# Four row tiles of the first norm from a second copy of x with channels on partitions, and another order of additions in the mixing's third phase

## The chip, the cores and the metric

One NeuronCore of a Trainium2 chip runs the whole block as one program. The metric is device time in microseconds (us), the median of several executions. Engines work side by side, each on its own list of instructions in a fixed order: TensorE (PE; its weight loads are shown apart as PEld), VectorE (DVE), ScalarE (ACT), GpSimd (POOL), and SyncE (SP), which here issues nearly all DMA transfers. They wait for each other by semaphores. TensorE's results go to PSUM, which this kernel uses as eight tiles (banks) of 128 x 512 float32 values; the other tiles lie in SBUF, 128 partitions wide.

## The reference

A transformer block with modulated norms, sequence 2048, width 448, 16 heads of 28, all in float32. Cut to what matters:

```python
mod = (silu(c) @ w_mod).reshape(1, 6, 1, -1)
sa, ca, ga, sb, cb, gb = (mod[:, i] for i in range(6))
h = layernorm(x) * (1 + ca) + sa                  # the first norm
x = x + ga * attention(h, wqkv, wo)               # 16 heads of 28
h = layernorm(x) * (1 + cb) + sb                  # the second norm
z = gelu(h @ w_in)                                # 2048 x 1792, two halves
z1, z2 = z[..., :896], layernorm(z[..., 896:])
g = w_sp @ z2 + b_sp[:, None]                     # 2048 x 2048: the mixing
x = x + gb * ((z1 * g) @ w_out)
```

## The kernel before

**Split operands.** Most operands of matmuls are kept as two tiles of the type fp32r: hi, a rounded copy, and lo, what the rounding left out. A product then takes hi x hi, lo x hi and hi x lo. The 448 channels fill three chunks of 128 and one of 64; the last holds hi in partitions 0 to 63 and lo in 64 to 127. `STEPS` is the order of the eleven matmuls of one output tile: their first index names the part of the activations (0, 1, 2 hi; 3, 4, 5 lo; 6 both of the last chunk), and runs 0, 2, 0, 2, 3, 5, 1, 1, 4, 6, 6.

**Stages.** First norm with the projections to Q, K and V; attention, head after head; output projection with the second norm; the two halves of z; the mixing; the last product. The program's order on each engine is the order of the code: nothing is reordered by a planner.

**The first norm.** Sequence rows come in four groups of 512 (four row tiles of 128). For a group, `ln_stat` takes mean and variance per row on VectorE, `ln_rs` makes 1/sqrt(var + eps) on GpSimd, `ln_norm` subtracts and scales on VectorE (rows on partitions; the last 64 channels are written twice, the second time by ScalarE). `ln_transpose` then turns the group on TensorE, sixteen 128 x 128 transposes into four PSUM banks, one per chunk of channels (L118). From each bank ScalarE makes scale ca and offset sa (L125) and the hi part (L132), and VectorE the lo part (L85). The result, `hT[g]`, has channels on partitions and feeds V (`v_tile`, one row tile, eleven matmuls, L273, then a copy by ScalarE, L277) and Q and K (`qk_unit`, one block of 128 rows of Q or K for one group, eleven matmuls, L288, then hi by ScalarE, L303, lo by VectorE, and two stores to DRAM, L309). Group 0 goes another way: `h_hi`, `h_off`, `h_lo` make hi straight from the transposed bank (L391), then offset minus hi (L397), and lo from the two (L401).

`ln_next(g)` is called while the tiles of group g - 1 are multiplied: it takes the statistics of the group after, transposes group g, and normalises the group after. Each loop round g = 1, 2, 3 is: two V tiles of group g, `ln_next(g + 1)`, two more V tiles, then the units m = 0 and 3 of the group. In round 3 these units come first, together with the clearing of the padded rows of the stacked Q and K tiles (L518 to L520) and the loads of head 0 (L529, L531).

**Banks.** Seven of the PSUM banks are dealt out by `bank` in a fixed cycle of two tags, s (three banks) and m (four); `turn` counts. A tile that gets a bank waits until the last reader of the bank's former tile is done.

**The mixing.** The 2048 x 2048 product is done with seven block products of one level of Strassen's scheme, in four phases p = 0 to 3, each in two halves of the output columns, each half in eight steps. In a step of phases 0 to 2 each of seven accumulators `acc[0..6]` gets three matmuls (L1224, L1225, L1226), in the order 0 to 6; in phase 3 there are four, 0, 1, 2, 6. After the eighth step `evac` adds the accumulators to the result blocks u11, u22 and so on (L1230 on VectorE), while TensorE begins the next half in new banks of the cycle. In phase 2 acc[0], acc[1], acc[2] are each added twice (u11 and u22), acc[3] to acc[5] once (u22), acc[6] once.

Of the kernel before, what the change touches and what calls it, by code (L numbers as in the profile page):

```python
# [8 lines left out]
F32 = mybir.dt.float32  # L9
F32R = mybir.dt.float32r  # L10
AF = mybir.ActivationFunctionType
ALU = mybir.AluOpType
# [4 lines left out]
S, D, H, DH, FH = 2048, 448, 16, 28, 896  # L17
# [3 lines left out]
NG = 4  # L21
# [9 lines left out]


@with_exitstack
def tile_adaln_mha_gmlp(ctx, tc, x, wqkv, wo, w_in, w_spT, b_sp, w_out, cT, w_mod, w_late, out):
    nc = tc.nc
    ctx.enter_context(tc.manual_schedule())
    pe, dve, act, pool, sp = nc.tensor, nc.vector, nc.scalar, nc.gpsimd, nc.sync
# [7 lines left out]
    m_scr = scr.tile([H, 2, S], F32, name="m_scr")  # L45
# [5 lines left out]
    ident = const.tile([128, 128], F32, name="ident")  # L51
# [6 lines left out]
    cols = {}  # L58
# [11 lines left out]
    hT = [hview(heapD[g // 2], g % 2 * 3584, 7, 512) for g in range(NG)]  # L70
# [35 lines left out]
    def rstd_of(var, rs, n):  # L106

        pool.tensor_scalar(out=rs, in0=var, scalar1=EPS, scalar2=None, op0=ALU.add)
        pool.tensor_tensor(out=rs, in0=rs, in1=mhalf[:, :n], op=ALU.pow)
# [35 lines left out]
    turn = [0]  # L145
# [12 lines left out]
    e1 = early.enter_context(tc.tile_pool(name="e1", bufs=2))  # L158
# [5 lines left out]
    def bank(name, kind=None):  # L164

        if kind is None:
            kind = "smsmsmm"[turn[0] % 7]
            turn[0] += 1
        return ring.tile([128, 512], F32, name=name, tag=kind, bufs=3 if kind == "s" else 4)
# [69 lines left out]
    mv1, xn1 = {}, {}  # L239

    def ln_stat(g, ts):
        if g not in mv1:
            mv1[g] = e1.tile([128, 4, 2], F32, name="mv"), e1.tile([128, 4], F32, name="rs")
        for t in ts:
            st = e1.tile([128, 6], F32, name="st", bufs=4)
            dve.bn_stats(out=st, in_=xts[4 * g + t])
            dve.bn_aggr(out=mv1[g][0][:, t, :], in_=st)

    def ln_rs(g, a, e):
        mv, rs = mv1[g]  # L250
        rstd_of(mv[:, a:e, 1], rs[:, a:e], e - a)

    def ln_norm(g, ts):
        mv, rs = mv1[g]
        for t in ts:
            xn = e1.tile([128, 512], F32, name="xn", bufs=4)
            dve.tensor_scalar(
                out=xn[:, :D],
                in0=xts.pop(4 * g + t),
                scalar1=mv[:, t, 0:1],  # L260
                scalar2=rs[:, t : t + 1],
                op0=ALU.subtract,
                op1=ALU.mult,
            )
            act.activation(xn[:, D:], xn[:, 384:D], AF.Copy)
            xn1.setdefault(g, []).append(xn)
# [15 lines left out]
    def qk_unit(ms, g, mid=None, later=None):  # L282
        pqs = [bank("pq") for _ in ms]
        for j, (a, b) in enumerate(STEPS):
            if mid and j in mid:
                mid[j]()
            for m, pq in zip(ms, pqs):
                pe.matmul(pq, wqk[:, b, m * 128 : (m + 1) * 128], hT[g][:, a, :], start=j == 0, stop=j == NST - 1)  # L288
        for m, pq in zip(ms, pqs):
            hi = stage.tile([128, 512], F32R, name="qh")  # L290
            lo = stage2.tile([128, 512], F32R, name="ql")
            if later is not None:
                f = stage.tile([128, 512], F32, name="qf")
                dve.tensor_copy(f, pq)  # L294
                later.append((qk_rest, (m, g, f, hi, lo)))
                continue
            if mid:
                f = stage.tile([128, 512], F32, name="qf")
                act.activation(f, pq, AF.Copy)
                act.activation(hi, f, AF.Copy)  # L300
                sub(pool, lo, f, hi)
            else:
                act.activation(hi, pq, AF.Copy)  # L303
                sub(dve, lo, pq, hi)
            qk_store(m, g, hi, lo)
# [180 lines left out]
    ln_rs(1, 2, 4)  # L486
    ln_norm(1, (2, 3))
    load_x(3, sp)
    ln_stat(2, range(4))
    turn[0] = 5  # L490
    qk_unit((0, 3), 0)
# [1 line left out]

    def ln_next(g):

        if 1 < g < NG - 1:
            ln_stat(g + 1, range(4))
            ln_rs(g + 1, 0, 4)
        ln_transpose(xn1.pop(g), e1, hT[g], cols["ca"], cols["sa"], (act,) * 4, (dve,) * 4)
        if g + 1 < NG:  # L500
            ln_norm(g + 1, range(4))

    ln_next(1)
    qk_unit((1,), 0)
    qk_unit((2,), 0)
    for i in (0, 2, 1, 3):
        qk_part("b", i, dve)
    for g in range(1, NG):
        if g == 3:
            early.close()  # L510
            stk = att.enter_context(tc.tile_pool(name="stk", bufs=1))
            kq = [[stk.tile([128, S], F32R, name=f"{n}st{i}") for n in "kq"] for i in range(3)]
            kst, qst = [a[0] for a in kq], [a[1] for a in kq]
            npool = att.enter_context(tc.tile_pool(name="npool", bufs=2))

            def pads(i, eng):

                dve.memset(kst[i][64:128, :].bitcast(F32), 0.0)  # L518
                eng.memset(qst[i][64:128, :].bitcast(F32), 0.0)
                pool.memset(kst[i][64:86, :].bitcast(F32), 1.0)  # L520

            pads(0, dve)

            def load_head(h, c0=0, c1=S):
                k, q = kst[h % 3], qst[h % 3]
                if h > 2:
                    sp.dma_start(q[84:86, :].bitcast(F32), q[86:88, :].bitcast(F32))
                for r0, i in ((0, 0), (56, 1), (28, 0)):
                    sp.dma_start(k[r0 : r0 + 28, c0:c1].bitcast(F32), qk_scr[i][D + h * DH : D + (h + 1) * DH, c0:c1])  # L529
                for r0, i in ((0, 0), (28, 1), (56, 0)):  # L530
                    sp.dma_start(q[r0 : r0 + 28, c0:c1].bitcast(F32), qk_scr[i][h * DH : (h + 1) * DH, c0:c1])  # L531

            load_head(0, 0, 1536)
            for m in (0, 3):
                qk_unit((m,), g)
            load_head(0, 1536, S)
        v_tile(4 * g)
        v_tile(4 * g + 1)
        if g == 3:
            pads(1, pool)  # L540
            pads(2, pool)
        if g + 1 < NG:
            ln_next(g + 1)
        for k in range(2):
            v_tile(4 * g + 2 + k)
            if g == 2 and k == 0:
                turn[0] += 2
        if g < 3:
            for m in (0, 3):
                qk_unit((m,), g)  # L550
    def to_row(cols4, i, *kind):
        n = cols4.shape[0]
        tp = bank("mtp", *kind)
        pe.transpose(tp[0:4, 0:n], cols4, ident[0:n, 0:n])
        nf = npool.tile([2 * NT, 128], F32, name="nf", bufs=1)
        dve.tensor_copy(nf[0:4, 0:n], tp[0:4, 0:n])
        sp.dma_start(m_scr[0, i, 0 : 4 * n].rearrange("(c p) -> c p", p=n), nf[0:4, 0:n])
# [657 lines left out]
    acc = {}  # L1215
# [13 lines left out]
    def d_add(dst, a, b, op=ALU.add):  # L1229
        dve.tensor_tensor(out=dst, in0=a, in1=b, op=op)  # L1230

    def evac(p, x):
        for f in range(3):
            i = 2 * f + x
            if p == 0:
                act.activation(u22[i], acc[f], AF.Copy)
            elif p == 1:
                act.activation(u21[i], acc[f], AF.Copy)
                d_add(u11[i], u11[i], acc[f])
            elif p == 2:  # L1240
                d_add(u11[i], u11[i], acc[f])
                d_add(u22[i], u22[i], acc[f])
            else:
                d_add(u11[i], u11[i], acc[f])
        for f in range(3):
            i = 2 * f + x
            if p == 0:
                d_add(u12[i], u22[i], acc[3 + f])
                act.activation(u11[i], acc[3 + f], AF.Copy, scale=-1.0)
            elif p == 1:  # L1250
                d_add(u21[i], u21[i], acc[3 + f])
                d_add(u22[i], u22[i], acc[3 + f], ALU.subtract)
            elif p == 2:
                d_add(u22[i], u22[i], acc[3 + f])
        if p == 0:
            act.activation(dq[x], acc[6], AF.Copy)
        elif p == 1:
            d_add(dq[x], dq[x], acc[6], ALU.subtract)
        elif p == 2:
            d_add(u6[x], dq[x], acc[6])  # L1260
        else:
            d_add(dq[x], acc[6], dq[x], ALU.subtract)

    bt, z1s = {}, {}

# [186 lines left out]
```

## Time and profile before

| | |
|---|---|
| median of 3 runs | 1398.27 us (1398.25 to 1399.03) |
| the profiled execution | 1399.65 us, span 1397.8 us |
| TensorE matmuls busy | 1391.5 us, 7187 instructions |
| VectorE busy | 1012.1 us |
| ScalarE busy | 774.8 us |
| GpSimd busy | 351.3 us |
| transposes of the first norm's groups 1 to 3 (L118, xn) | 48, starting from 31.2 to 59.8 us |
| attention | about 84 to 889 us |
| mixing | about 1080 to 1308 us |

The span is the time from the first to the last instruction of one profiled execution; the execution's own time has the start and end around it. A row of a timeline gives start, duration (both us), engine, line, operation, output and inputs, shape, how many instructions were put together, and in brackets how long the engine had stood idle before and who ended that. Durations of matmuls overlap, since they are pipelined: their pace is read from starts.

### The profile page before, as it was taken

How to read it: one execution, taken by the hardware profiler on the slowest of the kernel's cores; microseconds unless marked ns; L12 is line 12 of the kernel's file. 1: busy time of each engine (PE TensorE's matmuls, PEld its weight loads, DVE VectorE, ACT ScalarE, POOL GpSimd, SP SyncE). 2: the span in 40 equal slices, each digit the busy share in tenths (PEclk: the TensorE clock that was granted, in tenths of full speed). 3: DMA queues.
4: the chain of work that ended last, by engine and by line, in shares of the span. 5: the costliest groups of instructions: out<-in, count | busy, mean ns of one | idle time of the engine just before them, and what ended most of it. 6: DMA issues, size and time to landing. Idle time of an engine off the chain costs nothing.

```text
span 1397.8 us, 20319 instructions
## 1 busy us (share of the span) xinstructions
PE 1391.5 (100%) x7187; PEld 989.6 (71%) x7187; DVE 1012.1 (72%) x1738; ACT 774.8 (55%) x1491; POOL 351.3 (25%) x452
## 2 busy tenths in 40 slices
PE   9999999999999999999999999999999999999998
PEld 8888655555555555555555555988998888888888
DVE  7588888888888888888888851750366655667473
ACT  5623677777766666767777778363234544334110
POOL 2043315332435254423221231000142430000000
PEclk9999999999999999999999999999999999999999
DMA  7364744666565556655334212434103333446353
GB/s 224 111 193 150 204 116 158 176 181 171 163 178 173 172 172 190 176 165 158 112 94 115 61 51 72 163 120 140 46 11 103 113 113 107 144 140 214 134 176 105
DMA packets 104406, 194.59 MB, mean 139 GB/s; under 512 B 17302, under 2 KB 34718, under 8 KB 101758
## 3 DMA queue, kind: packets, MB, share of 16 engines
q1 hardware_dynamic: 101874, 189.45, 44.7%
q10 hardware_dynamic: 2430, 3.84, 0.7%
q8 instruction: 56, 0.92, 0.3%
q14 instruction: 46, 0.38, 0.1%
HBM read 134.78 MB, written 53.67 MB: 135 GB/s over the span
## 4 chain that ended last, share of the span: by engine, by line
PE 98%; DVE 1%; ACT 0%; issue 0%; POOL 0%; POOLq 0%
PE st_ps L649 18%; PE o_ps L664 17%; PE mt L584 17%; PE acc L1224 6%; PE acc L1225 6%; PE acc L1226 6%; PE z_ps L1150 5%; PE z_ps L1036 5%; PE pq L288 5%; PE wo_ps L906 3%; PE pv L273 2%; PE y_ps L1326 2%; PE y_ps L1325 2%; PE y_ps L1327 2%; PE tp L118 1%; PE wu L237 1%
## 5 line engine op out<-in xcount | busy, mean ns | idle before, releaser
L589 DVE TENSOR_REDUCE pm<-mt 128x1 f32<-128x512 f32 x1024 | 631.1, 680 | 82.6 <-PE mt L584 82.2
L653 ACT ACTIVATE P<-st_ps 128x512 f32<-128x512 f32 x1024 | 514.6, 632 | 205.6 <-PE st_ps L649 205.6
L649 PE MATMUL st_ps<-qst,kst 128*128 128x512 f32 x1024 | 404.3, 406 | 0.2 <-DVE qf L294 0.2
L584 PE MATMUL mt<-kst,qst 128*128 128x512 f32 x1024 | 403.4, 394 | 0.1
L649 PEld LDWEIGHTS st_ps<-qst,kst 128*128 128x128 f32 x1024 | 191.3, 188 | 136.0 <-issue 92.2
L664 PE MATMUL o_ps<-P,V 128*32 128x512 f32 x2048 | 247.1, 598 | 0.0
L584 PEld LDWEIGHTS mt<-kst,qst 128*128 128x128 f32 x1024 | 192.4, 188 | 37.7 <-DVE pm L589 5.3
L792 POOL TENSOR_TENSOR ws_raw<-ws_raw 128x512 f32<-128x512 f32 x80 | 103.2, 1290 | 287.0 <-DMA ws_raw<-in_w_spT_dram 280.7
L1112 ACT ACTIVATE wsp_h<-raw_sp 128x512 fp32r<-128x512 f32 x112 | 70.2, 632 | 163.0 <-PE acc L1226 120.3
L85 DVE TENSOR_TENSOR wsp_l<-raw_sp,wsp_h 128x512 fp32r<-128x512 f32 x112 | 80.5, 729 | 90.8 <-ACT wsp_h L1112 90.1
L664 PEld LDWEIGHTS o_ps<-P,V 128*32 128x32 f32 x2048 | 54.7, 109 | 122.6 <-issue 114.9
L1224 PE MATMUL acc<-wsp_h,heapA 128*128 128x512 f32 x224 | 87.4, 390 | 0.1
L1225 PE MATMUL acc<-wsp_l,heapA 128*128 128x512 f32 x224 | 87.2, 389 | 0.0
L1226 PE MATMUL acc<-wsp_h,heapA 128*128 128x512 f32 x224 | 87.2, 389 | 0.0
L1226 PE MATMUL acc<-wsp_h,heapB 128*128 128x512 f32 x174 | 67.7, 389 | 0.0
L1225 PE MATMUL acc<-wsp_l,heapB 128*128 128x512 f32 x174 | 67.7, 389 | 0.0
L1224 PE MATMUL acc<-wsp_h,heapB 128*128 128x512 f32 x174 | 67.7, 389 | 0.0
L288 PE MATMUL pq<-heapD,heapD 128*128 128x512 f32 x196 | 62.1, 390 | 0.0
L1154 DVE BATCH_NORM_STATS2 stz<-z 128x6 f32<-128x448 f32 x32 | 19.9, 625 | 50.4 <-ACT z L1153 29.8
L1224 PEld LDWEIGHTS acc<-wsp_h,heapA 128*128 128x128 f32 x224 | 42.0, 188 | 9.4 <-DVE cD L1230 0.9
L1226 PEld LDWEIGHTS acc<-wsp_h,heapA 128*128 128x128 f32 x224 | 42.1, 188 | 8.8
L1225 PEld LDWEIGHTS acc<-wsp_l,heapA 128*128 128x128 f32 x224 | 42.1, 188 | 8.5
(223 smaller groups left out, 1646.3 us busy)
## 6 DMA issues: line engine op xcount, KB each, us to landing
ws_raw<-in_w_spT_dram SPq DMA_DIRECT2D x160, 256.0 KB
ws_scr<-ws_raw SPq DMA_DIRECT2D x80, 256.0 KB
raw_sp<-ws_scr SPq DMA_DIRECT2D x80, 256.0 KB
kst<-qk_scr SPq DMA_DIRECT2D x45, 224.0 KB
qst<-qk_scr SPq DMA_DIRECT2D x45, 224.0 KB
raw_sp<-in_w_spT_dram SPq DMA_DIRECT2D x32, 256.0 KB
qk_scr<-qh SPq DMA_DIRECT2D x28, 256.0 KB
qk_scr<-ql SPq DMA_DIRECT2D x28, 256.0 KB
```

What stands on the lines that cost most here:

```text
L85: eng.tensor_tensor(out=dst, in0=a, in1=hi.bitcast(F32), op=ALU.subtract)
L288: pe.matmul(pq, wqk[:, b, m * 128 : (m + 1) * 128], hT[g][:, a, :], start=j == 0, stop=j == NST - 1)
L584: pe.matmul(mt, qst[h % 3][:, t * 128 : (t + 1) * 128], kst[h % 3][:, kb * 512 : (kb + 1) * 512], start=True, stop=True)
L589: dve.tensor_reduce(out=pms[h][:, t, kb : kb + 1], in_=mt, axis=AX.X, op=ALU.max)
L649: pe.matmul(st, kst[h % 3][:, kt * 128 : (kt + 1) * 128], qst[h % 3][:, qb * 512 : (qb + 1) * 512], start=True, stop=True)
L653: act.activation(p, st, AF.Exp, scale=SCALE)
L664: pe.matmul(otile[h][32 * qb : 32 * qb + 32, :], V[:, kt, h, :], ptiles.pop((u, qb)), start=kt == 0, stop=kt == NT - 1)
L792: pool.tensor_tensor(out=a, in0=a, in1=b, op=SUMS[i // 16][2])
L1112: act.activation(hi, raw, AF.Copy)
L1224: pe.matmul(acc[i], zh, hi, start=st == 0, stop=False)
L1225: pe.matmul(acc[i], zh, lo, start=False, stop=False)
L1226: pe.matmul(acc[i], zl, hi, start=False, stop=st == 7)
```

## The change

**In the first norm.** Group 3 no longer goes through `ln_norm` and `ln_transpose`. A second copy of its rows of x, laid out with channels on partitions (four tiles 128 x 512, the last with its 64 channels twice), is an input; SP loads it behind x of group 3, into the buffers of the first weights. x of group 3 is still loaded by rows, for the statistics alone. `ln_cols` makes 1/sqrt(var + eps) and mean times that, four columns each, in one tile of eight columns. `ln_rows`, behind unit 0 of group 1, transposes the eight columns on TensorE (one small transpose), copies them on VectorE and stores them to DRAM; `ln_bcast`, behind unit 3, reads them back as two tiles, each a row of 512 spread over 128 partitions, into buffers of xn. `ln_direct(c)` then makes a chunk: x times the first row on GpSimd, minus the second on VectorE, hi with scale and offset on ScalarE, offset minus hi on ScalarE, lo from both on VectorE. In round 2, chunks 0 and 2 stand behind V tile 10, chunks 1 and 3 behind V tile 11. The count `turn` is moved on so that the later banks fall as before.

**In the mixing.** In phase 2 `evac` adds acc[0] (twice), then acc[3], acc[4], acc[5], acc[6], then acc[1] and acc[2] (twice each).

```diff
     load_x(3, sp)
+    xcs = []
+    for c in range(4):
+        xcs.append(e1.tile([128, 2 * D], F32, name="xc", tag="wm", bufs=4)[:, :512])
+        sp.dma_start(xcs[c], xT[c])
     ln_stat(2, range(4))
@@ ln_next
-        if 1 < g < NG - 1:
-            ln_stat(g + 1, range(4))
-            ln_rs(g + 1, 0, 4)
+        if g == 2:
+            ln_stat(3, range(4))
+            ln_cols()
         ln_transpose(xn1.pop(g), e1, hT[g], cols["ca"], cols["sa"], (act,) * 4, (dve,) * 4)
-        if g + 1 < NG:
+        if g < 2:
             ln_norm(g + 1, range(4))
+
+    sr = e1.tile([128, 8], F32, name="sr", bufs=1)
+    rows3 = []
+
+    def ln_cols():
+        mv = mv1[3][0]
+        rstd_of(mv[:, :, 1], sr[:, 0:4], 4)
+        pool.tensor_tensor(out=sr[:, 4:8], in0=mv[:, :, 0], in1=sr[:, 0:4], op=ALU.mult)
+
+    def ln_rows():
+        tp = bank("tp")
+        pe.transpose(tp[0:8, 0:128], sr, ident)
+        st = e1.tile([8, 128], F32, name="srt", bufs=1)
+        dve.tensor_copy(st, tp[0:8, 0:128])
+        sp.dma_start(m_scr[1, 0, 0:1024].rearrange("(c p) -> c p", p=128), st)
+
+    def ln_bcast():
+        for i in range(2):
+            rows3.append(e1.tile([128, 512], F32, name="xn", bufs=4))
+            r = m_scr[1, 0, i * 512 : (i + 1) * 512].rearrange("(o n) -> o n", o=1)
+            sp.dma_start(rows3[i], r.broadcast_to([128, 512]))
+
+    def ln_direct(c):
+        x, sc, bi = xcs[c], cols["ca"][:, c : c + 1], cols["sa"][:, c : c + 1]
+        pool.tensor_tensor(out=x, in0=x, in1=rows3[0], op=ALU.mult)
+        dve.tensor_tensor(out=x, in0=x, in1=rows3[1], op=ALU.subtract)
+        hi = hT[3][:, c if c < 3 else 6, :]
+        act.activation(hi, x, AF.Identity, scale=sc, bias=bi)
+        r, d = (slice(0, 128), 3 + c) if c < 3 else (slice(64, 128), 6)
+        f = e1.tile([128, 512], F32, name="hfull")
+        act.activation(f[r], hi[r].bitcast(F32), AF.Identity, scale=-1.0, bias=bi[r])
+        dve.scalar_tensor_tensor(out=hT[3][r, d, :], in0=x[r], scalar=sc[r], in1=f[r], op0=ALU.mult, op1=ALU.add)
@@ the loop over g
-        if g + 1 < NG:
-            ln_next(g + 1)
+        if g == 1:
+            ln_next(2)
+        elif g == 2:
+            turn[0] += 3
         for k in range(2):
             v_tile(4 * g + 2 + k)
-            if g == 2 and k == 0:
-                turn[0] += 2
+            if g == 2:
+                turn[0] += 2 * (1 - k)
+                ln_direct(k)
+                ln_direct(2 + k)
         if g < 3:
             for m in (0, 3):
                 qk_unit((m,), g)
+                if g == 1:
+                    (ln_bcast if m else ln_rows)()
@@ evac
-        for f in range(3):
+        for f in range(1 if p == 2 else 3):
             i = 2 * f + x
...
+        if p == 2:
+            for f in (1, 2):
+                i = 2 * f + x
+                d_add(u11[i], u11[i], acc[f])
+                d_add(u22[i], u22[i], acc[f])
@@ kernel()
+    xT = _np.asarray(inputs["A_x"])[0, 1536:].T[rows].reshape(4, 128, 512)
```

More of the change, by code (lines that the diff above doesn't have):

```diff
@@ L33, in tile_adaln_mha_gmlp @@
 @with_exitstack
-def tile_adaln_mha_gmlp(ctx, tc, x, wqkv, wo, w_in, w_spT, b_sp, w_out, cT, w_mod, w_late, out):
+def tile_adaln_mha_gmlp(ctx, tc, x, wqkv, wo, w_in, w_spT, b_sp, w_out, cT, w_mod, w_late, xT, out):
     nc = tc.nc
@@ L1438 @@
         "w_late": w_late,
+        "xT": xT,
     }
```

## The prediction

> **What bounds the kernel now.** I read the page first, then the sums of busy time by stage, then the timelines of single engines around the two places that the change touches.
>
> ```profile
> span 1397.8 us, 20319 instructions
> PE 1391.5 (100%) x7187; PEld 989.6 (71%) x7187; DVE 1012.1 (72%) x1738; ACT 774.8 (55%) x1491; POOL 351.3 (25%) x452
> 58.00:84.00 26.00, 26.00 (x132) 22.96 (x131) 12.76 (x13) 11.11 (x19) 8.59 (x5) 1.00 0.49 145
> 84.00:889.00 805.00, 804.64 (x4417) 483.88 (x4416) 667.99 (x1138) 544.80 (x1073) 266.42 (x352) 1.00 0.50 149
> 1080.00:1308.00 228.00, 227.88 (x1006) 188.43 (x1005) 141.57 (x215) 91.77 (x160) 27.35 (x23) 1.00 0.44 139
> ```
>
> TensorE stands still for almost nothing in any stage: in the rows by stage (stretch and length, then busy time of PE, PEld, DVE, ACT and POOL, granted clock, DMA) it lacks 0.36 us of 805 in attention. So there is no slack anywhere behind the first norm that could take up or give back time: whatever TensorE gains or waits at one place moves the end by as much. The question is only how much work leaves TensorE, and where it now has to wait.
>
> **The 16 transposes.** The timeline of TensorE around group 3 of the first norm:
>
> ```profile
> 53.70 4.65 PE L273 MATMUL pv<-wv,heapD 128*128 128x448 f32 x22
> 58.19 1.91 PE L118 MATMUL tp<-ident,xn 128*128 128x128 f32 x16
> 59.85 4.73 PE L273 MATMUL pv<-wv,heapD 128*128 128x448 f32 x22
> 69.42 0.84 PE L288 MATMUL pq<-heapD,heapD 128*128 128x512 f32 x3
> 83.37 0.26 PE L554 MATMUL mtp<-ident,silu 112*4 112x112 f32 x1
> 83.40 0.48 PE L288 MATMUL pq<-heapD,heapD 128*128 128x512 f32 x1
> 83.72 0.40 PE L584 MATMUL mt<-kst,qst 128*128 128x512 f32 x1
> ```
>
> The sixteen hold the queue from 58.19 to the next V tile at 59.85: 1.66 us, removed. One small transpose (the eight statistics columns) is added. Its nearest row is L554: from 83.37 to the score matmul at 83.72 are 0.35 us, of which the projection matmul between them takes 0.23 (three in 0.84 and one in 0.39, so they start 0.23 apart). So +0.12. Net **-1.54**. The Trainium skill ("TensorE: Matmul & The Clock Gate", Part 4) gives about 275 ns for a transpose in a kernel's context; 15 fewer at that price would be -4.1 by an estimate from the page, and the whole sum 2.6 us lower. The row decides: 1.66 us for sixteen is 104 ns each, since they overlap.
>
> **What takes their place, and when it is ready.** The first reader of group 3 is the projection unit that starts at 69.42; with 1.54 us less ahead of it, at 67.88. Its steps read the parts in the order 0, 2, 0, 2, 0, 2, 1, 1, 1 and then, as tenth and eleventh, the part of channels 384 to 447. Tenth step: 67.88 + 9 x 0.227 = 69.92. By then this chain has to be through, in program order on each engine: per chunk a product on GpSimd, a subtraction on VectorE, two activations on ScalarE, a scalar_tensor_tensor on VectorE; four chunks, 0, 2, 1, 3. VectorE takes the next chunk's subtraction only behind the previous chunk's last operation, so chunks do not overlap. Group 0 has the same last three steps (h_hi, h_off, h_lo) and shows the prices:
>
> ```profile
> 22.14 0.78 ACT L391 ACTIVATE heapD<-tp,col_sa,col_ca 128x512 fp32r<-128x512 f32 x1
> 22.95 0.72 ACT L397 ACTIVATE hfull<-heapD,col_sa 64x512 f32<-64x512 f32 x1
> 23.70 0.76 DVE L401 SCALAR_TENSOR_TENSOR heapD<-tp,col_ca,hfull 64x512 fp32r<-64x512 f32 x1 [0.80 <-ACT hfull L397]
> 21.63 0.75 DVE L401 SCALAR_TENSOR_TENSOR heapD<-tp,col_ca,hfull 128x512 fp32r<-128x512 f32 x1 [0.23 <-ACT hfull L397]
> 22.30 0.61 DVE L85 TENSOR_TENSOR wv<-raw,wv 64x448 fp32r<-64x448 f32 x1
> 51.76 0.69 DVE L85 TENSOR_TENSOR heapD<-hfull,heapD 64x512 fp32r<-64x512 f32 x1 [0.64 <-ACT heapD L132]
> 58.38 0.54 ACT L277 ACTIVATE V<-pv 128x448 f32<-128x448 f32 x1 [1.54 <-PE pv L273]
> 58.83 0.78 ACT L125 ACTIVATE hfull<-tp,col_sa,col_ca 128x512 f32<-128x512 f32 x1
> ```
>
> First activation to second 0.81, second to VectorE 0.75, that to the next VectorE operation 0.67, a subtraction 0.69 and the hand-over 0.03 (from the end of L397 to L401): 2.95 a chunk (2.89 if the first one, here from SBUF, takes 0.72 as L397 does). The start: on ScalarE the copy of V tile 10 stands ahead of chunk 0. That tile's eleven matmuls run from 58.31 to 60.55 (22 take 4.49 above), its copy starts 0.19 behind them as at 58.38, and the next activation 0.45 later: 61.19. Chunk 3 then begins at 61.19 + 3 x 2.95 = 70.04, its VectorE operation 1.56 later, and its result is there at 72.4; by 2.89 at 72.1. TensorE waits 72.4 - 69.9. I take **+2.4** (bounds of the rows 2.2 and 2.5). Channels 128 to 255, needed at 69.7, are there at 69.4. So the transposes' 1.54 is more than given back.
>
> **What must be in time for that.** The two broadcast rows must land by about 59 for the first subtraction to end by 61.19 (a product 1.49 as in the row at 25.44, a subtraction 0.7).
>
> ```profile
> 52.48 1.79 DVE L257 TENSOR_SCALAR xn<-xg,mv,rs 128x448 f32<-128x448 f32 x4
> 54.47 0.96 ACT L277 ACTIVATE V<-pv 128x448 f32<-128x448 f32 x2
> 55.94 0.32 SPq L309 DMA_DIRECT2D qk_scr<-qh  x1
> 57.57 0.41 SPq L309 DMA_DIRECT2D qk_scr<-ql  x1
> 60.00:61.00 1.00, 1.00 (x7) 0.93 (x7) 0.69 (x1) 0.97 (x3) 0.00 (x0) 1.00 0.19 57
> 39.00:40.00 1.00, 1.00 (x6) 0.88 (x6) 0.97 (x2) 0.00 (x0) 0.00 (x0) 1.00 0.00 0
> 49.09 1.32 POOL L109 TENSOR_TENSOR rs<-rs,mhalf 128x4 f32<-128x4 f32 x1
> L624 POOL TENSOR_TENSOR w_late<-w_late 128x7 f32<-128x7 f32 x16 | 3.3, 208 | 1.2
> 25.44 1.49 POOL L85 TENSOR_TENSOR heapF<-raw,heapD 128x512 fp32r<-128x512 f32 x1 [14.66 <-ACT heapD L96]
> 76.36 1.24 SPq L531 DMA_DIRECT2D qst<-qk_scr  x3
> ```
>
> Without ln_norm(3) (the row at 52.48, and the four copies it holds up) ScalarE's V copies start at 51.7 (where its last hi ends, just ahead of the row at 51.76) instead of 54.47, and the stores around ln_rows issue 2.75 earlier: 53.2 to 55.4 instead of 55.94 to 57.98. The statistics' store goes between them, at about 54.3; the first broadcast follows the last store on SP's queue, at 55.8. The four stores of before, 1 MB, were through shortly after 60, less than 3 us behind the last issue; by that the rows land at 58 to 59: in time, with little over. If each came 1 us later the chain would move by as much. GpSimd's other products run ahead of VectorE, 1.49 against 2.95 a chunk: nothing. The eight columns are ready when the power at 49.09 ends, 50.41, plus one product (0.21 by L624; at most 1.32): 50.6 to 51.8, against TensorE's arrival at 51.2. I take 0; the bound is 0.6. The four loads of transposed x add 1 MB behind x of group 3; the DMA engines stand idle in the row at 39.00 and have room for it, and where the stores of the first unit land so late that the next unit's copies wait for their buffers, it is some tenths, in front of hT[2], which TensorE reads from 53.70 on: I take nothing. SP's loads of head 0 are issued by 77.6 before (the last row); behind later Q and K stores and memsets they move by some 2.7 us to 80.3, and the first score matmul by 0.9 to 84.6, 4.3 us behind, where the four queued stores took less than 3: nothing.
>
> **The order of additions.** Each of the seven accumulators of a half returns to its own bank in the next half: seven banks are dealt out in turn, seven at a time. Before, VectorE empties accumulators in the order 0, 1, 2, 3, 4, 5, 6 (two additions each for 0, 1, 2); after, 0, 3, 4, 5, 6, 1, 2. TensorE wants them back as 0, 1, 2, ..., three matmuls (0.68 us) apart.
>
> ```profile
> 1239.99 0.68 DVE L1230 TENSOR_TENSOR cE<-cE,acc 128x512 f32<-128x512 f32 x1
> 1245.37 0.68 DVE L1230 TENSOR_TENSOR cF<-cE,acc 128x512 f32<-128x512 f32 x1
> 1242.67 0.39 PE L1224 MATMUL acc<-wsp_h,heapA 128*128 128x512 f32 x1
> 1243.35 0.39 PE L1224 MATMUL acc<-wsp_h,heapA 128*128 128x512 f32 x1
> 1278.69 0.68 DVE L1230 TENSOR_TENSOR cE<-cE,acc 128x512 f32<-128x512 f32 x1
> 1284.08 0.68 DVE L1230 TENSOR_TENSOR cD<-cC,acc 128x512 f32<-128x512 f32 x1
> 1281.44 0.40 PE L1224 MATMUL acc<-wsp_h,heapA 128*128 128x512 f32 x1
> 1282.42 0.50 PE L1224 MATMUL acc<-wsp_h,heapA 128*128 128x512 f32 x1
> ```
>
> Ten additions, 0.60 apart. First boundary: the eighth now frees accumulator 1, at 1239.99 + 7 x 0.60 + 0.68 = 1244.86 and a hand-over of 0.05, where TensorE wants it at 1243.35: 1.55 us. It then wants accumulator 2 at 1244.91 + 0.68 = 1245.59; the tenth addition ends at 1246.05: 0.5 more, **+2.07**. Second boundary: accumulator 1 is free at 1278.69 + 4.19 + 0.68 = 1283.56, wanted at 1281.44; accumulator 2 is free at 1284.76, so its first matmul starts at 1284.81 where before it started at 1282.42 (that one already waited 0.3): **+2.39**. What VectorE has queued behind (splits of the next weights) starts at the same time in both orders. The bounds are those of the hand-over, 4.3 and 4.7.
>
> **Sum.** -1.66 + 0.12 + 2.4 + 2.07 + 2.39 = +5.32. The profiled execution (1399.65, span 1397.8) would become 1404.97 with a span of 1403.1; it lies 1.38 over the median of the runs, so I apply the sum to the median: 1398.27 + 5.32 = **1403.6**.
>
> **Rivals.**
>
> - *The direct path is in time.* If hi-part, offset and subtraction of neighbouring chunks overlapped, or the chunk cost under 2.1 us, nothing waits at 69.92: 1398.27 - 1.54 + 4.46 = 1401.2. For it: VectorE and ScalarE lose the four norms and copies of group 3. Against: the strict order of VectorE. Chance 0.10.
> - *The additions come early enough (the other side, not slower).* If the two batches of additions began 1.5 and 2.2 us earlier against TensorE, accumulator 1 would be free when wanted; that is the point from which it decides. Then -1.54 + 2.4 = +0.9, 1399.1. For it: TensorE hardly waits there now. Against: both batches run without a pause behind splits that TensorE's own progress releases. Chance 0.08; with the first rival together (1396.7) 0.03.
> - *The rows come late and TensorE goes cold.* Rows that land 1 us later make the wait 3.4 us, and a wait so long might cost speed afterwards. At the start TensorE ran small matmuls at a slow pace:
>
> ```profile
> 2.00:4.00 2.00, 2.00 (x11) 2.00 (x11) 1.31 (x3) 0.21 (x1) 1.55 (x2) 1.00 0.92 233
> 8.00:10.00 2.00, 2.00 (x20) 2.00 (x19) 1.93 (x6) 0.18 (x1) 0.44 (x2) 1.00 1.06 247
> ```
>
> 11 against 20 in 2 us, for some 5.5 us, though the granted clock reads 1.00: about 2.4 us lost, in all 1403.6 + 1.0 + 2.4 = 1407. The Trainium skill ("TensorE: Matmul & The Clock Gate", Part 1) has the half clock return after an idle window of about 3.4 us; by that rule my three waits, none above 2.5, leave the clock alone. No run here shows it. Chance 0.07.
>
> **How the numbers follow.** The forecast has 0.70 (its own range 1402.6 to 1404.6); 0.02 is for the rest. The range 1401.0 to 1405.8 takes in the first rival and the bounds of the waits, and leaves out the second and third. A measurement of this kernel tells a change of 0.2%, 2.8 us, from none, so slower begins at 1401.07: forecast, cold TensorE and half of the first rival, 0.82; the rest mostly within, 0.16.
>
> **What would show it.** L118 with 32 transposes of xn and one of sr; a wait of about 2.4 us of TensorE before the tenth step of its first unit on group 3, released by a VectorE scalar_tensor_tensor; four chunks about 2.9 us apart on VectorE; and at both boundaries of the third phase waits of 1.5 to 2.2 and 0.5 us at L1224's successor, released by VectorE additions. The prediction is wrong if TensorE shows no wait at one of these places, or one elsewhere.

## The result, and the profile after

The changed kernel takes 1406.48 us (median of 4 runs, 1404.78 to 1407.38) beside 1398.26 for the kernel before (4 runs, 1398.01 to 1399.03): 1.0056 times as long, with a 95% interval of 1.0039 to 1.0074. It is slower by 8.2 us, and lies above the predicted range. The profiled execution of after took 1406.49 with a span of 1404.7.

The head of the page of after:

```profile
span 1404.7 us, 20307 instructions
PE 1392.0 (99%) x7172; PEld 989.1 (70%) x7172; DVE 1014.4 (72%) x1739; ACT 775.2 (55%) x1487; POOL 360.5 (26%) x457
```

TensorE has fifteen instructions fewer and is busy 0.5 us longer, and the span grew by 6.9 us: the loss is waiting and slow running. In after, L513 is the product for the statistics columns, L517 the small transpose, L520 its store and L526 the reading back; L530, L531, L533, L536 and L537 are the five steps of `ln_direct` (product, subtraction, hi, offset minus hi, lo); L626, L1266 and L1272 are L584, L1224 and L1230 of before. V tiles 4 to 7 belong to group 1, 8 to 11 to group 2, 12 to 15 to group 3. To place the loss, the timeline of TensorE of both kernels is read from one common mark, the first V matmul that follows the last part of group 0 (L443; the two executions reach it 0.48 us apart, ahead of everything that changed). First before, then after:

```profile
24.51 1.89 PE L443 MATMUL pv<-wv,heapD 128*128 128x448 f32 x8 [0.32 <-DVE heapD L401]
44.13 2.08 PE L273 MATMUL pv<-wv,heapD 128*128 128x448 f32 x9
64.42 0.86 PE L288 MATMUL pq<-heapD,heapD 128*128 128x512 f32 x3
74.41 9.12 PE L273 MATMUL pv<-wv,heapD 128*128 128x448 f32 x44
```

```profile
24.03 1.89 PE L443 MATMUL pv<-wv,heapD 128*128 128x448 f32 x8 [0.32 <-DVE heapD L401]
44.86 4.76 PE L273 MATMUL pv<-wv,heapD 128*128 128x448 f32 x22 [0.93 <-DVE ql L85]
52.50 0.27 PE L517 MATMUL tp<-ident,sr 128*8 128x128 f32 x1 [0.38 <-POOL sr L513]
64.19 0.86 PE L288 MATMUL pq<-heapD,heapD 128*128 128x512 f32 x3
69.20 0.87 PE L288 MATMUL pq<-heapD,heapD 128*128 128x512 f32 x3
70.79 0.50 PE L288 MATMUL pq<-heapD,heapD 128*128 128x512 f32 x1 [0.27 <-DVE heapD L537]
72.24 0.50 PE L288 MATMUL pq<-heapD,heapD 128*128 128x512 f32 x1 [0.94 <-ACT heapD L533]
73.78 0.49 PE L288 MATMUL pq<-heapD,heapD 128*128 128x512 f32 x1 [0.81 <-DVE heapD L537]
76.77 1.22 PE L288 MATMUL pq<-heapD,heapF 128*128 128x512 f32 x2 [2.49 <-DVE heapD L537]
81.96 9.13 PE L273 MATMUL pv<-wv,heapD 128*128 128x448 f32 x44
91.27 0.40 PE L626 MATMUL mt<-kst,qst 128*128 128x512 f32 x1
```

| from the mark to | before | after | lost so far |
|---|---|---|---|
| V tile 6 (44.13; 44.86) | 19.62 | 20.83 | 1.21 |
| unit 0 of group 2 (64.42; 64.19) | 39.91 | 40.16 | 0.25 |
| unit 0 of group 3 (69.42; 69.20) | 44.91 | 45.17 | 0.26 |
| V tile 12 (74.41; 81.96) | 49.90 | 57.93 | 8.03 |
| first score matmul (83.72; 91.27) | 59.21 | 67.24 | 8.03 |

The first 1.2 us come in front of V tile 6, 0.8 more up to V tile 8, around the small transpose (0.38 of it marked as a wait), and then the sixteen transposes that are gone give 1.75 back (this term is read alone in the last experiment). Between unit 0 and V tile 12 of group 3 go 7.8 us. Unit 0's tenth step would stand at 69.20 + 9 x 0.227 = 71.24 and came at 76.77: 5.5 us in four waits instead of one of 2.4. (The brackets add up to 4.51 only: they begin where the matmul before has ended, and starts that follow each other at 0.227 overlap matmuls of 0.39 to 0.50.) From there thirteen matmuls to V tile 12 take 5.19 us instead of 13 x 0.227 = 2.95: another 2.24, which is no wait. The stretches show what it is (the column after the five busy times is the granted clock):

```profile
72.00:74.00 2.00, 0.95 (x3) 0.48 (x3) 1.02 (x2) 0.91 (x2) 0.00 (x0) 1.00 0.00 0
74.00:76.00 2.00, 0.28 (x1) 0.00 (x0) 0.37 (x2) 1.58 (x3) 0.00 (x0) 0.63 0.00 0
78.00:79.00 1.00, 1.00 (x3) 0.78 (x3) 0.52 (x2) 0.00 (x0) 0.00 (x0) 0.50 0.81 299
81.00:82.00 1.00, 1.00 (x5) 0.77 (x5) 1.00 (x1) 0.00 (x0) 1.00 (x1) 0.83 0.00 0
```

The clock falls to 0.50 during the last wait and is back only in the row at 81.00.

Why the operands are late, from the timelines of the other engines of after:

```profile
43.48 0.60 ACT L303 ACTIVATE qh<-pq 128x512 fp32r<-128x512 f32 x1 [1.69 <-DMA qk_scr<-qh]
51.76 0.69 POOL L513 TENSOR_TENSOR sr<-mv,sr 128x4 f32<-128x4 f32 x1
55.51 0.35 SPq L520 DMA_DIRECT2D m_scr<-srt  x1
57.91 0.80 SPq L526 DMA_DIRECT2D xn<-m_scr  x2
61.68 5.51 POOL L530 TENSOR_TENSOR xc<-xc,xn 128x512 f32<-128x512 f32 x4 [9.24 <-DMA xn<-m_scr]
63.02 1.76 DVE L531 TENSOR_TENSOR xc<-xc,xn 128x512 f32<-128x512 f32 x1 [6.27 <-POOL xc L530]
66.42 1.32 DVE L537 SCALAR_TENSOR_TENSOR heapD<-xc,col_ca,hfull 128x512 fp32r<-128x512 f32 x1 [1.65 <-ACT hfull L536]
69.98 0.75 DVE L537 SCALAR_TENSOR_TENSOR heapD<-xc,col_ca,hfull 128x512 fp32r<-128x512 f32 x1 [1.64 <-ACT hfull L536]
...
75.96 0.75 DVE L537 SCALAR_TENSOR_TENSOR heapD<-xc,col_ca,hfull 64x512 fp32r<-64x512 f32 x1 [1.63 <-ACT hfull L536]
```

The broadcasts are issued at 57.9, and GpSimd starts at 61.68, when the first row is there. The first subtraction takes 1.76 and the first L537 1.32 while GpSimd is in its four products (61.68 to 67.19); the next ones 0.68 and 0.75. From chunk to chunk it is 3.56 us once and then 2.99 twice (69.98 to 75.96), and the last ends at 76.7.

In the mixing, first VectorE's additions and then TensorE's matmuls of after, at the first boundary (two rows of each) and the second:

```profile
1250.15 0.68 DVE L1272 TENSOR_TENSOR cF<-cE,acc 128x512 f32<-128x512 f32 x1
1251.34 0.68 DVE L1272 TENSOR_TENSOR cD<-cD,acc 128x512 f32<-128x512 f32 x1
...
1289.39 0.68 DVE L1272 TENSOR_TENSOR cD<-cC,acc 128x512 f32<-128x512 f32 x1
```

```profile
1249.64 0.39 PE L1266 MATMUL acc<-wsp_h,heapA 128*128 128x512 f32 x1
1250.33 0.39 PE L1266 MATMUL acc<-wsp_h,heapA 128*128 128x512 f32 x1
...
1288.93 0.50 PE L1266 MATMUL acc<-wsp_h,heapA 128*128 128x512 f32 x1 [0.31 <-DVE cD L1272]
1290.12 0.50 PE L1266 MATMUL acc<-wsp_h,heapA 128*128 128x512 f32 x1 [0.23 <-DVE cD L1272]
```

The new accumulator 1 starts at 1250.33, 0.69 behind accumulator 0 and without a wait, while the old accumulator 1 is read for the last time only from 1251.34 on. At the second boundary the fourth accumulator comes some 0.7 later than before against the first, and from the start of phase 3 to the end of the span it is still 116.94 us against 117.05 before. From the first score matmul to the first boundary it is 1158.37 against 1158.95 before. So the whole loss lies ahead of 82 us: the 8.03, less the 0.48 by which after is early at the mark and some 0.6 behind it, are the 6.9 of the span.

### The profile page after: what moved, and what is told of

It reads as the page before. It is cut to its first block, busy times and chain, and to the rows that moved or that the text cites. A ratio compares the mean times of both kernels' runs of the same rounds, so it can differ in the third digit from the quotient of the medians.

```text
span 1404.7 us, 20307 instructions
## 1 busy us (share of the span) xinstructions
PE 1392.0 (99%) x7172; PEld 989.1 (70%) x7172; DVE 1014.4 (72%) x1739; ACT 775.2 (55%) x1487; POOL 360.5 (26%) x457
## 4 chain that ended last, share of the span: by engine, by line
PE 92%; DMA 3%; DVE 2%; ACT 1%; issue 1%; POOL 0%; SPq 0%; ACTq 0%; DVEq 0%; POOLq 0%
PE st_ps L691 18%; PE o_ps L706 17%; PE mt L626 17%; PE acc L1266 6%; PE acc L1267 6%; PE acc L1268 6%; PE z_ps L1192 5%; PE z_ps L1078 5%; PE pq L288 3%; PE wo_ps L948 3%; PE y_ps L1373 2%; PE y_ps L1374 2%; PE y_ps L1372 2%; DMA raw_sp<-ws_scr 1%; PE pv L273 1%
## 5 line engine op out<-in xcount | busy, mean ns | idle before, releaser
L626 PE MATMUL mt<-kst,qst 128*128 128x512 f32 x1024 | 402.6, 393 | 0.1
L626 PEld LDWEIGHTS mt<-kst,qst 128*128 128x128 f32 x1024 | 192.4, 188 | 38.3 <-DVE pm L631 2.7
L1266 PE MATMUL acc<-wsp_h,heapA 128*128 128x512 f32 x224 | 87.5, 391 | 0.5 <-DVE cD L1272 0.5
L1266 PE MATMUL acc<-wsp_h,heapB 128*128 128x512 f32 x174 | 67.7, 389 | 0.0
L1266 PEld LDWEIGHTS acc<-wsp_h,heapA 128*128 128x128 f32 x224 | 42.0, 188 | 10.5 <-DVE cD L1272 1.8
```

Of the source, the lines that this page charges most:

```text
L626: pe.matmul(mt, qst[h % 3][:, t * 128 : (t + 1) * 128], kst[h % 3][:, kb * 512 : (kb + 1) * 512], start=True, stop=True)
L1266: pe.matmul(acc[i], zh, hi, start=st == 0, stop=False)
```

## Experiments

In the expectations, theory A is the reading above throughout: the additions cost nothing, and the first norm loses by the loads of transposed x, by late rows, by VectorE slowed beside GpSimd, by chunks that do not overlap, and by the clock, each as measured there. The rival is named in each expectation.

Each change of a median is against the kernel before as it ran beside that kernel on the same chip (1398.26 for after, 1398.54 for the next four, 1398.07 for the last four). "Place" is the change in the time from the mark at L443 to V tile 12, from one profile each (49.90 before).

| kernel | median us | change | ratio, 95% interval | place |
|---|---|---|---|---|
| after | 1406.48 | +8.2 | 1.0056 [1.0039, 1.0074] | +8.03 |
| additions alone | 1398.31 | -0.2 | 0.9999 [0.9990, 1.0008] | +0.05 |
| first norm alone | 1407.03 | +8.5 | 1.0059 [1.0045, 1.0072] | +8.19 |
| TensorE kept busy | 1404.44 | +5.9 | 1.0044 [1.0030, 1.0057] | +5.82 |
| transposed x loaded later | 1404.88 | +6.3 | 1.0045 [1.0032, 1.0059] | +6.57 |
| rows early | 1402.25 | +4.2 | 1.0031 [1.0019, 1.0043] | +4.80 |
| products on VectorE | 1406.52 (one run) | +8.5 | none | +7.25 |
| ... and chunks overlapped | 1398.82 | +0.8 | 1.0004 [0.9996, 1.0013] | +0.47 |
| ... and transposed x later | 1397.35 | -0.7 | 0.9994 [0.9985, 1.0004] | -1.31 |

Place and median agree within 0.7 us in all but the one that ran once. So the place can be read where the intervals of the medians overlap.

### The two halves of the change, each alone

The kernel before with the new `evac`; and after with the old one:

```diff
 # additions alone: before, with
-        for f in range(3):
+        for f in range(1 if p == 2 else 3):
...
+        if p == 2:
+            for f in (1, 2):
+                i = 2 * f + x
+                d_add(u11[i], u11[i], acc[f])
+                d_add(u22[i], u22[i], acc[f])
 # first norm alone: after, without these
```

> Only the order of additions is changed, the first norm is that of before. Theory A (the bank that an accumulator gets is the one whose last reader comes first in the program, so the new order of readings carries the banks with it): TensorE waits some tenths at the two boundaries as it did before, 1398.3 within 0.7. Theory B (each accumulator goes back to its own bank, as the prediction had it): waits of 2.1 and 2.4 us at the two boundaries, 1402.7.

> Only the first norm is changed, the additions stand in the order of before. Theory A (all of the loss sits in the first norm): as the changed kernel, 1406 within 1.5. Theory B (the additions cost 4.5 us of it): 1402. If the additions in the new order gain something by themselves, this one is slower than the changed kernel by as much.

1398.31 and 1407.03: the additions cost nothing that the times can tell, and the first norm all. The one wait of TensorE in the mixing with the additions alone (total, times, longest):

```profile
PE acc L1224 <- DVE cD L1230: 0.2, 1, 0.2
```

### TensorE kept busy

Twenty matmuls whose result nobody uses, in front of the units of group 3:

```diff
+            wd = ps_o.tile([128, 512], F32, name="wd", tag="o")
+            for _ in range(20):
+                pe.matmul(wd, wqk[:, 0, 0:128], hT[2][:, 0, :], start=True, stop=True)
             for m in (0, 3):
                 qk_unit((m,), g)
             load_head(0, 1536, S)
```

> The changed kernel with twenty matmuls without use (128x512, 4.5 us) put in front of TensorE's first unit of group 3, where it waits 5.5 us in all. Theory A (the wait halves TensorE's clock, and the thirteen matmuls behind it then start 0.43 us apart instead of 0.23): granted clock 1.00 between 74 and 82 us, spacing 0.23 us, 2.2 us less than the changed kernel, 1404.2. Theory B (the wide spacing comes from something else at that place, such as transfers or the memsets): spacing 0.43 us as in the changed kernel, and no gain, 1406.5.

1404.44, and the place 2.21 us earlier than in after. The timeline of TensorE and a stretch:

```profile
69.62 4.70 PE L572 MATMUL wd<-heapD,heapD 128*128 128x512 f32 x20
77.17 0.72 PE L288 MATMUL pq<-heapD,heapF 128*128 128x512 f32 x2 [0.82 <-DVE heapD L537]
80.27 4.03 PE L273 MATMUL pv<-wv,heapD 128*128 128x448 f32 x19
```

```profile
78.00:80.00 2.00, 2.00 (x10) 1.66 (x9) 1.52 (x2) 0.47 (x1) 0.00 (x0) 1.00 0.95 327
```

The operands are no earlier, and TensorE still cannot pass its tenth step before 77.17; but with 4.5 us of useless work in place of most of the waiting the clock stays at 1.00, and the thirteen matmuls take 80.27 - 77.17 = 3.10 instead of 5.19. So 2.1 to 2.2 us of the loss are the clock, and they follow from standing still (the transfers and the clearing beside them are those of after).

### Transposed x loaded later

```diff
-    xcs = []
-    for c in range(4):
-        xcs.append(e1.tile([128, 2 * D], F32, name="xc", tag="wm", bufs=4)[:, :512])
-        sp.dma_start(xcs[c], xT[c])
     ln_stat(2, range(4))
     turn[0] = 5
     qk_unit((0, 3), 0)
+    xcs = []
+    for c in range(4):
+        xcs.append(e1.tile([128, 2 * D], F32, name="xc", tag="wm", bufs=4)[:, :512])
+        sp.dma_start(xcs[c], xT[c])
```

> The changed kernel with the four loads of transposed x issued behind the four stores of the first unit instead of ahead of them. Theory A (the loads hold up the stores, these hold up ScalarE's and VectorE's copies into the same buffers by 1.7 us, and with them TensorE at V tile 6, the statistics and the two rows): no wait at V tile 6, none or 0.1 at the small transpose, the rows land 1.2 to 1.7 us earlier, the chain of chunks ends 1.2 to 1.7 earlier; 1404.5 to 1405.5. Theory B (the rows are late for another reason): TensorE gains 1.7 us at V tile 6 and the small transpose and loses them again in front of group 3, 1406.5.

1404.88, place +6.57, 1.5 us less than after. V tile 6 and the small transpose no longer wait. In after the 1 MB of transposed x stands ahead of the first unit's stores; ScalarE waits for a store's buffer (the row at 43.48), so the lo half behind it is late, and V tile 6 needs the bank that this lo reads. The chain runs as before, only earlier (this kernel reaches the mark at 23.28, 0.75 ahead of after):

```profile
59.13 5.50 POOL L530 TENSOR_TENSOR xc<-xc,xn 128x512 f32<-128x512 f32 x4 [9.16 <-DMA xn<-m_scr]
74.20 1.22 PE L288 MATMUL pq<-heapD,heapF 128*128 128x512 f32 x2 [2.49 <-DVE heapD L537]
```

From the mark, the rows come 59.13 - 23.28 = 35.85 behind it instead of 61.68 - 24.03 = 37.65: 1.8 us earlier, and TensorE gets to unit 0 of group 3 1.7 earlier too (66.71 - 23.28 = 43.43 against 45.17), so the waits in front of group 3 hardly shrink. The thirteen matmuls up to V tile 12 (at 79.75) take 5.55 us here, 0.36 more than in after.

### Rows early

The two broadcast rows are read from an input ahead of unit 0, without the way through DRAM. Their values are not the statistics.

```diff
-            r = m_scr[1, 0, i * 512 : (i + 1) * 512].rearrange("(o n) -> o n", o=1)
-            sp.dma_start(rows3[i], r.broadcast_to([128, 512]))
+            sp.dma_start(rows3[i], xT[0][i : i + 1, :].broadcast_to([128, 512]))
...
+        if g == 1:
+            ln_bcast()
         if g < 3:
             for m in (0, 3):
                 qk_unit((m,), g)
-                if g == 1:
-                    (ln_bcast if m else ln_rows)()
+                if g == 1 and m == 0:
+                    ln_rows()
```

> The changed kernel with the two spread rows read from the transposed x instead of from the stored statistics, and read ahead of unit 0 of group 1, so that no store and read through DRAM stands in front of GpSimd's products (the normalised values of group 3 are wrong, all work and sizes are the same). Theory A (the chain begins late because the rows land at 61.7, and because VectorE's first two operations beside GpSimd's products take 1.8 and 1.3 us): products done by 58, first subtraction 0.7, the chain begins behind the copy of V tile 10 at 62.7 and ends at 73.9; TensorE, there at 71.2, waits 2.7 us instead of 5.5, and the clock stays at 1.00; 1401.5. Theory B (the chunks behind each other are what counts, whenever the rows land): the chain ends about where it did, 1405.5 to 1406.5.

1402.25, some 0.7 above the 1401.5 that was expected, and not for the reason of a longer wait:

```profile
73.22 0.75 DVE L536 SCALAR_TENSOR_TENSOR heapD<-xc,col_ca,hfull 64x512 fp32r<-64x512 f32 x1 [1.63 <-ACT hfull L535]
```

```profile
74.02 0.73 PE L288 MATMUL pq<-heapD,heapF 128*128 128x512 f32 x2 [2.48 <-DVE heapD L536]
```

```profile
72.00:74.00 2.00, 0.00 (x0) 0.00 (x0) 0.75 (x1) 1.94 (x4) 0.00 (x0) 1.00 0.00 0
74.00:76.00 2.00, 1.98 (x6) 1.60 (x7) 1.52 (x3) 0.29 (x1) 0.00 (x0) 0.66 0.58 216
76.00:78.00 2.00, 2.00 (x7) 1.51 (x6) 1.62 (x2) 0.60 (x1) 0.18 (x1) 0.50 1.07 298
```

With rows in time there is the one wait that the prediction described, at the tenth step and nearly of its size: unit 0 starts at 69.26, its tenth step would stand at 71.30 and came 2.72 later (2.48 in the bracket), where 2.4 was predicted. GpSimd's products are early, from 52.49 to 57.99. The first subtraction again ran beside them and took 1.84 us, where 0.7 was expected, but at no cost, since the chain begins behind the copy of V tile 10 (62.64). The clock goes to 0.50 all the same, 0.6 us after TensorE has gone on, and the thirteen matmuls up to V tile 12 (at 78.71) take 4.69 us, 1.74 more than at full clock.

### Products on VectorE

```diff
-        pool.tensor_tensor(out=x, in0=x, in1=rows3[0], op=ALU.mult)
+        dve.tensor_tensor(out=x, in0=x, in1=rows3[0], op=ALU.mult)
```

> The changed kernel with the four products on VectorE instead of GpSimd, the order of the rest as it was. Theory A (a subtraction and a scalar_tensor_tensor of VectorE are slowed by GpSimd's products beside them): the first subtraction takes 0.68 and not 1.76, the first scalar_tensor_tensor 0.75 and not 1.32; the chunks are 3.6 us apart instead of 3.0, and the chain ends within 0.7 of where it did. Theory B (the first subtraction is long because its second row lands late): 1.7 again.

1406.52 in one run, so only its trace is used. VectorE and TensorE:

```profile
62.55 0.69 DVE L531 TENSOR_TENSOR xc<-xc,xn 128x512 f32<-128x512 f32 x1
64.89 0.75 DVE L537 SCALAR_TENSOR_TENSOR heapD<-xc,col_ca,hfull 128x512 fp32r<-128x512 f32 x1 [1.64 <-ACT hfull L536]
```

```profile
76.85 1.22 PE L288 MATMUL pq<-heapD,heapF 128*128 128x512 f32 x2 [3.21 <-DVE heapD L537]
```

Without GpSimd's products beside them the same two operations take 0.69 and 0.75 instead of 1.76 and 1.32. What that saves the first chunk, the product on VectorE takes back in each: the chunks are 3.72 apart and the tenth step comes 0.2 us earlier than in after, by the mark. The place is better by 0.8, since TensorE ran slowly for a shorter time: the thirteen matmuls take 4.62 us (to 81.47) instead of 5.19.

### Chunks overlapped

Products on VectorE, and the steps of neighbouring chunks interleaved, so that VectorE has the next chunk's first two operations to do while ScalarE works on this one's hi and offset:

```diff
                 turn[0] += 2 * (1 - k)
-                ln_direct(k)
-                ln_direct(2 + k)
+                for fn, c in (
+                    ((ln_pre, 0), (ln_pre, 2), (ln_hi, 0), (ln_hi, 2), (ln_lo, 0), (ln_pre, 1), (ln_lo, 2)),
+                    ((ln_hi, 1), (ln_pre, 3), (ln_lo, 1), (ln_hi, 3), (ln_lo, 3)),
+                )[k]:
+                    fn(c)
```

`ln_pre` is product and subtraction, `ln_hi` the two activations, `ln_lo` the last step. The second kernel has the later loads of above as well.

> The changed kernel with the products on VectorE and its operations in another order, so that chunks overlap: product and subtraction of chunks 0 and 2 first, then the last operation of 0, product and subtraction of 1, the last of 2, product and subtraction of 3, the last of 1 and of 3. Theory A (four chunks of 3 us in a row are the wait; overlapped, ScalarE's two activations set the pace, 1.5 us a chunk): chain begins at 63.1, ends at 70.9, TensorE is there at 71.2 and does not wait, clock 1.00; 1398.7. Theory B (the late rows alone are the cause): a wait of 3 us or more remains, 1402 to 1404.

> The one before with the loads of transposed x behind the stores of the first unit as well. Theory A: no wait at V tile 6 nor at the small transpose nor in front of group 3 (up to 0.5 there), what is left is the gain of the transposes, 1.5 us under the time before: 1397.0. Theory B: TensorE, earlier by 1.7 us, waits for the chain instead, 1398.7 as the one before.

1398.82 and 1397.35. With the chunks overlapped, the last step of the chain (timeline of VectorE), and the waits of TensorE that are left (total, times, longest):

```profile
70.59 0.75 DVE L546 SCALAR_TENSOR_TENSOR heapD<-xc,col_ca,hfull 64x512 fp32r<-64x512 f32 x1 [0.97 <-ACT hfull L541]
```

```profile
PE pv L273 <- DVE ql L85: 1.1, 1, 1.1
PE tp L517 <- POOL sr L513: 0.4, 1, 0.4
```

The same chain that ended at 76.7 now ends at 71.3, no wait is left in front of group 3, and 7.6 us are back (place +0.47 instead of +8.03). The rows are as late as in after: the first product starts at 61.81, 37.60 behind the mark against 37.65. So late rows cost no wait once the chunks overlap. The overlap with the products left on GpSimd was not run. With the loads later too, TensorE's timeline has none of these waits:

```profile
43.48 4.73 PE L273 MATMUL pv<-wv,heapD 128*128 128x448 f32 x22
53.27 9.13 PE L273 MATMUL pv<-wv,heapD 128*128 128x448 f32 x44
62.24 0.86 PE L288 MATMUL pq<-heapD,heapD 128*128 128x512 f32 x3
72.40 9.12 PE L273 MATMUL pv<-wv,heapD 128*128 128x448 f32 x44
```

Here the bare exchange can be read. From V tile 8 to unit 0 of group 2: 62.24 - 53.27 = 8.97 against 64.42 - 53.70 = 10.72 before, -1.75 for the sixteen transposes. From V tile 6 to V tile 8, with the small transpose: 9.79 against 9.57, +0.22. Unit 0 to V tile 12 of both groups: 10.16 against 9.99, +0.17. In the timeline this last kernel reaches V tile 12 1.3 us ahead of before. Its median is 0.7 lower, with an interval that includes no change: the fastest of all, and not shown to be faster than before.

## Why the prediction was right and wrong

**Right.** *What bounds it:* the 8.03 us that TensorE had lost by its first score matmul are 6.9 in the span and 8.2 in the medians; what lies behind took up 0.6 at most. *The transposes and the small one:* -1.66 and +0.12, measured -1.75 and +0.22. *The chain:* strictly one chunk after another, 2.99 apart once GpSimd is through (2.95 predicted), with the last operation deciding the tenth step; in the kernel with rows early the tenth step came 2.72 late where 2.4 was predicted. *The sign*, and that the transposes' gain would be more than given back. But the sign came out by other terms than forecast: of the 5.32, the first norm had 0.86 and the additions 4.46, and alone they cost 8.5 and nothing.

**Wrong: the additions.** +2.07 and +2.39 were predicted; alone they changed the time by -0.2 (-1.4 to +1.1 by the interval). The step that failed is "each of the seven accumulators of a half returns to its own bank". In the built program, the banks of accumulators 0 to 6 are, half by half:

```
before, halves of phases 0-2   0 6 4 1 3 2 5
after, phase 2, first half     0 3 5 2 4 1 6
after, phase 2, second half    0 4 6 2 3 1 5
after, phase 3, first half     0 3 5 2          (accumulators 0, 1, 2, 6)
```

One rule fits the whole table: within a tag, a new tile gets the bank whose last reader stands earliest in the program. Accumulators 0, 3 and 5 have one tag, 1, 2, 4 and 6 the other. After the change of order, 4 and 6 are read ahead of 1 and 2, so the new accumulator 1 gets the bank of the old 4, and the new 2 that of the old 6. The trace agrees: at the second boundary the new accumulator 2 starts at 1290.12, right behind the addition of the old accumulator 6 (1289.39 + 0.68 = 1290.07), and long before the old accumulator 2 is read (from 1291.18 on). What is left at this boundary is that the fourth accumulator starts 0.7 later against the first than before in after, and 0.3 later with the additions alone. The rival that had the additions early enough gave the right sum for this part by a mechanism that did not take place.

**Wrong: when the rows land.** "The rows land at 58 to 59" was 61.7. The stores on SP's queue go out later than reckoned (the statistics' at 55.51 instead of 54.3; the 55.4 beside it should have been 57.98 - 2.75 = 55.2), since ScalarE's copies ahead of them stand later too, behind the late V tile 6 (from 52.90 on instead of 51.7). The broadcasts are issued at 57.9 instead of 55.8: the prediction put them right behind the last store, but SP's queue waits another 0.8 us until the statistics' own store has landed. They then take 3.8 us to land instead of less than 3.

**Wrong: "GpSimd's other products ... nothing".** They were off the path by order, but slowed VectorE's first two operations by 1.07 and 0.57 us: 1.76 and 1.32 instead of 0.69 and 0.75 without them. The Trainium skill ("SBUF — State Buffer", section "SBUF: two separate sides") says that a VectorE operation with two inputs in SBUF and a GpSimd operation exclude each other at a shared pair of ports, the later one waiting for the whole instruction of the other. The two durations agree: what was added is at most one product of GpSimd (5.51 / 4 = 1.38). Both delays together make the chain end at 76.7 instead of 72.4: the first L537 ends at 67.74 where 63.5 was reckoned (61.19 + 1.56 + 0.75), 4.2 later. The rows account for 2.5 of it (61.68, a product of 1.34 and a subtraction of 0.69 make 63.7, where 61.19 was reckoned), the slow operations for 1.6. Of the 2.5, 1.4 would have come without late rows, since the copy of V tile 10 starts at 62.14 instead of 60.74. That part makes no wait: TensorE gets to group 3 later by about as much, at 69.20 instead of 67.88. So of the 3.1 us by which the wait was longer than forecast (5.5 instead of 2.4), the rows make some 1.1 and the slow operations 1.6.

**Wrong: "The four loads ... I take nothing".** The case was named (stores that land late, copies that wait for their buffers) and priced at some tenths; it was 1.21, in front of V tile 6 (a bank that a late copy still read) and not in front of hT[2]. Moving the loads took this wait and that of the small transpose away and brought the place 1.5 us nearer. The product of 128 x 4 values that the small transpose waits for took 0.69, inside the bounds taken (0.21 to 1.32) but not at the end that was chosen: the wait was 0.38, where 0 was taken.

**Wrong: the clock.** That it goes to half was in a rival with a chance of 0.07. What was predicted for that rival, late rows and a cold TensorE, is what happened in the first norm; its 1407 was near by luck, since it contains 4.46 for additions that cost nothing. The Trainium skill ("TensorE: Matmul & The Clock Gate", Part 1) has the half clock return after about 3.4 us of idleness, and I used it as a reason against. Here a single wait of 2.48 was followed by a granted clock of 0.50, with matmuls at half pace; the measurement decides.

**The rival "the direct path is in time".** Its condition, that the steps of neighbouring chunks overlap, is what decides: the two kernels that make them overlap have no wait in front of group 3. It had the gain of that at -1.54; the last kernel's place shows -1.31.

**The sum as measured**, at V tile 12, with the prediction's term in brackets: +1.21 in front of V tile 6 (0), +0.79 up to V tile 8 with the small transpose and its wait (+0.12), -1.75 for the transposes (-1.66), +5.53 of waiting (+2.4), +2.24 of slow clock (0): +8.02 (+0.86), against +8.03 in the table.

What stays open: what exactly sets the moment at which the clock falls. With the rows early it fell about 3.1 us after TensorE had stopped, when work had already begun again; in after it fell in the middle of a wait, after some 4 us in which TensorE had been busy somewhat under half the time. The traces narrow it, though no run was made to test it. The low clock lasted 3.41 us in two kernels (rows early, products on VectorE) and twice that, 6.83, in the other three that lost it (after, first norm alone, transposed x later). Laid off backwards from each fall in lengths of 3.41 us, the last length has TensorE busy for 0.28 to 1.43 us. A length with 2.05 us of work, the one before it in products on VectorE, brought no fall, and full clock came back behind the first length with 3.33 us or more. By these five falls it is the work within such a length that counts, not the length of a single wait.

## What to carry to other kernels

Work that leaves the bounding engine must be priced by when its replacement is ready, in the program order of each engine that makes it: here the same chain of operations cost 8 us in one order, and nothing that could be measured with its products on another engine and its chunks overlapped, though the rows were as late. A buffer's next user is a fact of the built program; whoever argues from "it returns to its own bank" should look it up, above all where the change is one of order. And a wait of 2.5 us on TensorE had a second price behind it in every kernel that had one (1.7 to 2.7 us of slow matmuls), so an estimate that ends in such a wait should add it.

## What the hardware showed unexpectedly

- The granted clock went to 0.50 with one wait of 2.48 us, and matmuls of 0.227 us pitch then ran 0.43 apart. Full clock came back 4.0 us (rows early, at 78.05) and 4.6 us (after, at 81.33) behind the end of the wait, which cost 1.7 and 2.2 us. Waits of 0.93 (V tile 6) and 0.82 (TensorE kept busy) left it alone. The low clock came in lengths of 3.41 us, once or twice.
- Beside GpSimd's products VectorE's subtraction took 2.6 times as long (1.76 / 0.69).
- A 4 KB store and its reading back as two broadcast rows took from 55.51 (issue) to 61.68, with stores of Q and K between them on the same queue: 6.2 us for 512 numbers twice.
